# Batch 0 of a linear-attention kernel: q transposed on TensorE as loaded, kv sums on array quarters

## The chip, the cores and the metric

The kernel runs on one core of a Trainium2 chip. The time is the device time of one execution in microseconds (us); the median of several executions stands for a kernel. The engines are TensorE (PE; its weight loads are shown apart as PEld), VectorE (DVE), ScalarE (ACT), GpSimd (POOL) and SyncE (SP), which issues nearly all transfers between device memory and the on-chip memory. TensorE writes its results into PSUM, from which DVE and ACT read.

## The reference

Attention with cosine weights, followed by a feed-forward network (FFN):

```python
r = np.maximum(x, 0.0)                                   # phi, for q and for k
phi(x) = np.concatenate([r * cos_w, r * sin_w], axis=-1) # angle = pi/2 * position / S
kv  = einsum('bhsf,bhsd->bhfd', phi(k), v)
num = einsum('bhsf,bhfd->bhsd', phi(q), kv)
den = einsum('bhsf,bhf->bhs', phi(q), sum_s phi(k))[..., None] + 1e-06
x   = (num / den), heads side by side: 4608 x 512
h   = x @ w_in                                           # 512 x 2048
out = np.maximum(0.01 * h, h) @ w_out                    # 2048 x 512
```

q, k and v are float32 of 8 batches x 8 heads x 576 positions x 64. Each batch's first 512 positions are one group for the FFN (groups 0 to 7); the last 64 positions of all batches make group 8.

## The kernel before, in words

The work is a long list of named steps. A string, `ORDER`, names them in the order in which they are issued; a letter behind a colon chooses the engine of a step (D, A or P), a number behind an @ the buffer or PSUM place. Each engine, and SP with its transfers, takes its own instructions strictly in that order, so a step that waits holds everything behind it on the same engine. Several transfers can be in flight at once, but a transfer whose target buffer is still being read holds back all later ones on SP.

The steps that matter for batch 0, by their names:

- `Lq0`, `Lk0`, `Lv0`, `Lq1`, `Lk1`, `Lv1` load q, k and v of batches 0 and 1; `lq2`, `lk2`, `lv2` and so on those of later batches; `Lw1.i` and `Lw2.i` load the FFN weights in parts. Loads land in float32 staging buffers, which several of them share by turns.
- `q0.j.hg.f` (`q_prep`, lines 376 and 382): relu and one angle, cos or sin, for position slot j and four heads, from float32 to float16. `qt0.j` (`q_transpose`, line 506) turns eight heads on TensorE against a float16 identity, and `qo0.j` copies the result from PSUM to `qpT`.
- `kp0` and `kc0` do the same for k (lines 420, 376 and 382), `v0.c` casts v (line 390 or 388), all into float16. k and v are laid out so that the two heads of a pair lie on the two halves of the 128 partitions.
- `kv0.hg` (`kv_sum`, line 440): for two pairs of heads, nine matmuls for each head add up k'v in PSUM. Each takes a 64 x 128 weight (64 positions, cos and sin features side by side) on one half of the array's rows. Two extra columns of ones give the sum of k'. `ko0.hg` (`kv_out`) copies the result.
- `n0.jp.hg` (`num_half`, line 558), `N0` (`divide`, lines 534 to 539), `xt0` (line 578) and `xo0` give the numerators, the division and the transposed FFN input for two position slots and four heads.
- `f0.m` (`ffn1`, line 603) and `e0` make the first product and its activation; `F0` (`ffn2`, line 626) the second. The first two groups are computed with plain products. Groups 1 to 8 use a seven-product scheme for the second product and groups 2 to 8 also for the first (lines 740 and 823); its weight sums `T1` and `T2` are two float16 tiles that are written only after batch 1.
- `i.n` are dummy matmuls on a blank tile (line 307), 15 ahead of the first real one and nine between the first steps.

Batch 1's transposes, sums and numerators (`qt1`, `kv1`, `n1`, `xt1`) are made on TensorE between the steps `F0`; batches from 2 on have q and x transposed by DMA.

Of the kernel before, what the change touches and what calls it, by code (L numbers as in the profile page):

```python
# [13 lines left out]
P = 128  # L14
# [17 lines left out]
Lq0.0@0 q0.0.0.1:A q0.1.0.1:A Lq0.1 q0.3.0.0:P q0.2.0.1:P q0.0.0.0:A q0.1.1.0:A q0.1.1.1:A  # L32
q0.3.1.1:A q0.1.0.0:A i.0@1 Lk0.0@1 Lk0.3 Lk0.2 Lk0.1 qt0.1@0 kp0.0.1 q0.3.1.0:D q0.3.0.1:P
kc0.6:P Lv0.0@2 Lv0.2 kc0.4:D Lv0.1 kc0.1:P kp0.1.0 kp0.2.1 kp0.1.1 q0.0.1.0:A kp0.0.0 v0.0:D
kc0.8:D kc0.3:P i.2@0 qo0.1:A i.3@1 q0.2.0.0:A Lw1.0@3 v0.2:P q0.0.1.1:A qt0.0@1 i.1@0 Lv0.3
kp0.3.1 v0.3:P kc0.2:P Lw1.3 q0.2.1.0:A kc0.5:A q0.2.1.1:A qt0.2 Lw1.7 qt0.3@0 i.7@1 i.4@0
c1.0:P i.8@1 c1.3:P i.6@0 qo0.0:A Lw1.1 Lw1.2 c1.2:P Lw1.4 kc0.7:A i.9@1 i.5@0 v0.1:A kv0.0@1
qo0.3:A ko0.0:A n0.0.0@0 N0.0.0 qo0.2:A n0.1.0 N0.1.0 kc0.0:A kv0.1@1 ko0.1:A xt0.0.0@1 n0.0.1@0
N0.0.1 c1.4:P xo0.0.0:A c1.1:A Lw1.5 Lw1.6 n0.1.1 N0.1.1 Lw1.8 xt0.1.0@0 xo0.1.0:D c1.8:D c1.5:D
f0.0.a@1 f0.2.a@0 Lw2.0@0 Lq1@2 q1.0.1:D q1.3.1:D q1.3.0:D q1.2.1:D Lk1.0 kp1.0.1 Lk1.1 c1.6:P  # L40
Lw2.1@1 f0.3.a kp1.1.1 Lw2.2@3 xt0.1.1@1 f0.1.a q1.0.0:D c1.7:P f0.4.a f0.5.a Lv1.0 xt0.0.1@0
w0.0:P w1.0:P xo0.0.1:A f0.0.b f0.2.c f0.1.b xo0.1.1:A f0.0.c q1.2.0:D f0.3.c Lw2.3.0 Lw2.3.2
f0.2.d f0.3.d f0.2.e f0.3.e f0.4.d f0.5.d f0.1.c f0.0.d f0.1.d f0.0.e e0.1 kp1.0.0 q1.1.0:D
W0.1:D f0.1.e e0.0 f0.6.a@0 f0.7.a f0.6.d f0.7.d e0.3 w0.2:A f0.14@1 f0.15 e0.7 f0.8@0 lq2@0
Lv1.1 f0.9 e0.2 e0.4 f0.10@1 f0.11 e0.5 qt1.3@0 qo1.3:A kc1.2:D F0.2.0 F0.2.2 q1.1.1:A F0.0.0@0
kc1.1:A F0.1.0@1 w1.2:D qt1.0@1 qo1.0:A f0.12@0 kp1.3.1 f0.13 qt1.2@1 qo1.2:A e0.6 kp1.1.0
F0.1.2 F0.0.2 kc1.6:A kc1.5:D v1.0:D F0.1.4 w2.0:A qt1.1@1 qo1.1:A F0.0.4 kc1.8:A w2.2:P v1.2:A
v1.3:A rq2 q2.2.0:P v1.1:D q2.0.0:P q2.3.1:A F0.0.6 kp1.2.1 F0.2.4 q2.3.0:A F0.2.6 kc1.4:D
F0.1.6 kc1.0:D w3.0:D kv1.0@0 ko1.0:D w3.2:D F0.0.8 F0.2.8 F0.0.10 kc1.3:D n1.1.0@1 F0.2.10
F0.2.12 F0.2.14 F0.3.0 n1.0.0@0 F0.0.12 F0.3.2 F0.3.4 W0.2:D T1 F0.3.6 F0.3.8 F0.3.10 F0.3.12  # L50
F0.3.14 O0.3:A@1 N1.1.0 kc1.7:D kv1.1@1 O0.2:D@2 q2.2.1:P F0.1.8 N1.0.0 ko1.1:D n1.0.1@0 N1.0.1
F0.0.14 q2.1.0:A O0.0:A@3 q2.0.1:A lk2@2 rk2 ks2.0:P lv2.0@1 lv2.1 xt1.0.0@1 xo1.0.0:A n1.1.1
q2.1.1:A kc2.0:A kc2.3:A F0.1.10 lq3@3 lk3@0 F0.1.12 qT2.0 xt1.0.1@0 N1.1.1 xo1.0.1:D kc2.6:A
xt1.1.0@0 xo1.1.0:D F0.1.14 ks2.3:A xt1.1.1@0 xo1.1.1:D f1.2.0@1 f1.0.0@0 f1.0.2 f1.1.0 kc2.5:A
f1.1.2 e1.0 v2.0:A v2.1:D ks2.2:D f1.4.0 f1.4.2 f1.2.2 f1.5.0 f1.5.2 e1.2 kc2.7:A ks2.8:A f1.3.0
ks2.5:P ks2.4:P f1.10@0 f1.11 e1.5 kc2.1:D ks2.7:P ks2.6:D kc2.8:D T3 ks2.1:D kc2.4:D kc2.2:P
kv2 T2 T4 f1.6@0 ko2:A n2.0 N2.0 f1.3.2 e1.1 rk3 kc3.2:D kc3.3:A f1.7 e1.3 ks3.7:A n2.1 ks3.1:A
f1.12@1 f1.13 qT2.1 N2.1 D0.3 S1.1a n2.2 rq3 q3.2.1:A e1.6 N2.2 q3.2.0:P S1.2a f1.8@0 f1.9 n2.3
N2.3 q3.1.0:A f1.14@1 O0.1:A@0 ks3.8:P q3.1.1:D f1.15 kc3.7:P F1.2.0.0@0 W0.4:D e1.4 S1.1b
F1.1.0.0@1 lq4@1 kc3.0:A e1.7 W1.1:D S1.3b S1.1c W1.3:D S1.2c F1.1.0.1 q3.0.0:P S1.3c F1.1.1.0  # L60
q3.0.1:A S1.2b lv3.0@2 lv3.1 F1.1.1.1 F1.2.0.1 F1.2.1.0 q3.3.0:A W0.3:D M1.1:A q3.3.1:A F1.2.1.1
O1.2@1 ks3.4:D kc3.6:A F1.6.0.0@1 F1.6.0.1 F1.6.1.0 F1.6.1.1 M1.6 xT2 ks3.2:D F1.5.0.0@0
F1.5.0.1 X2.1:D f2.0.1 ks3.5:A f2.1.1 kc3.5:A kc3.4:A v3.1:A v3.0:A qT3.0 f2.0.5 S1.3a F1.7.0.0
lk4@3 W1.2:D X2.2:D ks3.3:A S1.4b X2.3:D X2.4:D W1.4:P kc3.8:A b2.0:A rq4 F1.7.0.1 F1.7.1.0
f2.0.2 ks3.6:A F1.7.1.1 rk4 s2.0:A qT3.1 f2.0.3 q4.3.0:P kc3.1:A f2.0.6 ks3.0:A kv3 kc4.4:P
u2.0:D z2.0 a2.0 f2.0.7 D0.2 ko3:A e2.0 b2.1:A q4.2.1:P f2.1.5 n3.0 S1.4a q4.0.0:P kc4.6:P
F1.5.1.0 F1.5.1.1 f2.1.6 y2.0 s2.1:A f2.1.3 N3.0 f2.0.4 ks4.7:P kc4.2:P u2.1:A M1.7 z2.1 c2.0
lv4.0@2 n3.1 F1.4.0.0 N3.1 f2.1.2 lq5@0 d2.0 f2.2.1 f2.1.7 n3.2 e2.1 O1.5@2 a2.1 b2.2:A f2.2.5
y2.1 kc4.3:A D1.5 ks4.3:A s2.2:A N3.2 f2.2.2 f2.2.6 a2.2 f2.1.4 n3.3 F1.3.0.0 N3.3 u2.2:A f2.2.3
D0.1 z2.2 v4.0:P d2.1 c2.1 S2.1a ks4.8:A e2.2 f2.3.5 ks4.5:D f2.3.1 q4.0.1:P b2.3:A F1.3.0.1  # L70
F1.3.1.0 F1.3.1.1 O1.3@2 q4.3.1:P ks4.4:D kc4.1:P f2.2.7 f2.3.6 f2.3.2 y2.2 kc4.0:A s2.3:D
F1.4.0.1 u2.3:A f2.3.7 c2.2 F2.1.0.0@0 q4.1.1:A f2.2.4 d2.2 y2.3 f2.3.3 z2.3 a2.3 F1.4.1.0 xT3
X3.1:D X3.2:D f2.3.4 d2.3 F1.4.1.1 f3.0.1 f3.1.1 O1.4@0 q4.2.0:P f3.0.5 ks4.2:A X3.3:D X3.4:D
# [75 lines left out]
def kernel(  # L149
# [751 lines left out]
    def step(name, f, *args):  # L901
        steps[name] = f, args
# [192 lines left out]
```

## Time and profile before

| | |
|---|---|
| runs | 280.63, 280.81, 281.11 us; median 280.81 |
| the profiled execution | 281.11 us, span 279.2 us |
| busy, share of the span | PE 94%, DVE 78%, ACT 65%, POOL 41% |
| granted TensorE clock | 0.999 |
| transfers | 57.59 MB, 206 GB/s over the span |

A busy row counts the time in which an engine has an instruction at work. Matmuls overlap, so the pitch of a row of matmuls (its time without the last one's duration, divided by their number less one) is what one of them costs, not its mean duration. The idle time of an engine is shown with the event that ended it. A load is read by what was waiting for it.

### The profile page before, as it was taken

The page shows a single profiled execution, that of the slowest core. Times are in us where ns is not written, and L with a number is a line of the kernel's source. Part 1 is how long each engine was busy: PE and PEld are TensorE (multiplying, and loading weights), DVE is VectorE, ACT ScalarE, POOL GpSimd, SP SyncE. Part 2 cuts the span into 40 slices and gives each one's busy share as a digit, 9 for nine tenths or more (in the row PEclk, how much of TensorE's full clock was granted, in tenths as well). Part 3 has the DMA queues.
Part 4 walks back from the last instruction along what each step waited for, and adds up shares of the span by engine and source line. Part 5 has one row for each costly group of instructions (what it writes and reads, how often), then busy time and mean ns, then how long its engine had stood idle before and what let it go on. Part 6 is the DMA issues. An engine that isn't in the chain of part 4 may idle for free.

```text
span 279.2 us, 7172 instructions
## 1 busy us (share of the span) xinstructions
PE 263.1 (94%) x2904; PEld 221.3 (79%) x2904; DVE 216.6 (78%) x430; ACT 180.6 (65%) x320; POOL 114.7 (41%) x135
## 2 busy tenths in 40 slices
PE   7669989799998999999999999999999999999993
PEld 2457445456798889998999999999999989999982
DVE  1862589594989798978988989889897888677862
ACT  7945971597996869668868557663557645666300
POOL 5854153809039930495397250970623003100000
PEclk9999999999999999999999999999999999999999
DMA  7999999779999999999795998459548214220144
GB/s 238 350 393 388 409 390 380 277 196 231 287 231 228 267 216 174 312 245 284 112 301 133 252 215 288 80 113 216 128 77 179 86 35 119 75 77 0 40 123 102
DMA packets 77263, 57.59 MB, mean 206 GB/s; under 512 B 49456, under 2 KB 65840, under 8 KB 76848
## 3 DMA queue, kind: packets, MB, share of 16 engines
q1 hardware_dynamic: 76624, 56.63, 75.5%
q10 hardware_dynamic: 608, 0.52, 0.6%
q8 instruction: 22, 0.36, 0.5%
q14 instruction: 9, 0.07, 0.1%
HBM read 36.70 MB, written 9.44 MB: 165 GB/s over the span
## 4 chain that ended last, share of the span: by engine, by line
PE 76%; DMA 12%; DVE 4%; SPq 2%; POOL 1%; issue 1%; ACT 1%
PE ps L823 32%; PE ps_f L740 27%; PE ps_h L603 5%; DMA w2st<-in_moe_w_out_dram 4%; PE ps_o L626 4%; DMA wext<-in_moe_w_in_dram 4%; PE ps_kv L440 3%; PE ps_num L523 3%; DMA out_dram<-osb 2%; DMA vst<-in_v_dram 2%; SPq L256 2%; POOL w L390 1%; PE ps_f L823 1%; DVE y L656 1%; DVE osb L656 1%
## 5 line engine op out<-in xcount | busy, mean ns | idle before, releaser
L823 PEld LDWEIGHTS <-g 128*128 128x128 f16 x640 | 61.9, 98 | 7.3 <-ACT g L612 0.2
L764 ACT ACTIVATE g<-ps_f 128x512 f16<-128x512 f32 x84 | 48.5, 596 | 26.5 <-DVE ps_f L656 14.7
L823 PE MATMUL ps<-w,g 128*128 128x256 f16 x496 | 64.4, 273 | 0.0
L740 PEld LDWEIGHTS <-w 128*128 128x128 f16 x448 | 48.4, 114 | 2.0 <-issue 1.1
L740 PE MATMUL ps_f<-xT,w 128*128 128x256 f16 x336 | 48.2, 273 | 0.0
L740 PEld LDWEIGHTS <-wext 128*128 128x128 f16 x336 | 36.4, 114 | 2.2 <-issue 1.6
L823 PE MATMUL ps<-T,ext 128*128 128x256 f16 x240 | 32.6, 272 | 0.0
L603 PE MATMUL ps_h<-xT,w 128*128 128x512 f16 (+1 forms) x144 | 29.6, 356 | 0.6 <-DVE xs L539 0.6
L823 PEld LDWEIGHTS <-ext 128*128 128x128 f16 x256 | 24.7, 98 | 2.5
L740 PE MATMUL ps_f<-X,wext 128*128 128x256 f16 x176 | 26.0, 273 | 0.2 <-ACT ps_f L388 0.2
L603 PEld LDWEIGHTS <-w 128*128 128x128 f16 x144 | 15.6, 114 | 10.6 <-DVE xs L539 0.8
L656 DVE TENSOR_TENSOR ps_f<-ps_f,u 128x512 f32<-128x512 f32 x28 | 19.5, 695 | 5.3 <-PE ps_f L740 3.2
L370 POOL TENSOR_SCALAR kst<-kst 128x2304 f32<-128x2304 f32 x6 | 13.3, 2221 | 23.5 <-DMA kst<-in_k_dram 19.3
L764 ACT ACTIVATE g<-y 128x512 f16<-128x512 f32 x28 | 17.7, 634 | 7.7 <-DVE y L656 7.7
L656 DVE TENSOR_TENSOR y<-ps_f,s 128x512 f32<-128x512 f32 x28 | 19.1, 683 | 4.1 <-PE ps_f L740 2.6
L539 DVE TENSOR_TENSOR xs<-ps_num,rden 128x512 f16<-128x512 f32 x28 | 19.4, 691 | 1.0
L612 ACT ACTIVATE g<-ps_h 128x1024 f16<-128x1024 f32 x16 | 16.2, 1024 | 4.5 <-PE ps_h L603 4.3
L823 PE MATMUL ps<-ext,g 128*128 128x256 f16 x128 | 17.9, 273 | 0.0
L656 DVE TENSOR_TENSOR osb<-ps,ext 128x512 f32<-128x512 f32 x23 | 15.6, 685 | 2.7 <-PE ps L823 1.7
L740 PE MATMUL ps_f<-xT,wext 128*128 128x256 f16 x112 | 16.8, 273 | 0.9 <-ACT s L388 0.8
L740 PE MATMUL ps_f<-X,w 128*128 128x256 f16 x112 | 16.8, 273 | 0.7 <-DVE y L656 0.6
L388 ACT COPY s<-ps_f 128x512 f32<-128x512 f32 x19 | 11.2, 587 | 9.4 <-PE ps_f L740 3.6
(121 smaller groups left out, 476.4 us busy)
## 6 DMA issues: line engine op xcount, KB each, us to landing
out_dram<-osb SPq DMA_DIRECT2D x32, 256.0 KB, 3.7
qst<-in_q_dram SPq DMA_DIRECT2D x7, 1024.0 KB, 10.6
kst<-in_k_dram SPq DMA_DIRECT2D x6, 1152.0 KB, 7.2
vst<-in_v_dram SPq DMA_DIRECT2D x12, 576.0 KB, 6.8
w2st<-in_moe_w_out_dram SPq DMA_DIRECT2D x3, 1024.0 KB, 12.9
ext<-in_moe_w_in_dram SPq DMA_DIRECT2D x4, 512.0 KB, 11.2
kst<-in_k_dram SPq DMA_DIRECT2D x4, 288.0 KB, 5.7
vst<-in_v_dram SPq DMA_DIRECT2D x4, 288.0 KB, 6.6
```

The lines of the kernel that those rows point to most:

```text
L370: POOL.tensor_scalar(out=t, in0=t, scalar1=FMAX, scalar2=0.0, op0=ALU.min, op1=ALU.max)
L388: nc.scalar.copy(o, i)
L440: nc.tensor.matmul(ps[:, o, (c - lo) * NE : (c - lo + 1) * NE], lhsT=st["kp", b][sl, c, j, :], rhs=vm[sl, c, j, :], start=(j == 0), stop=( ...
L523: nc.tensor.matmul(ps[lo:hi, h // 4, (h % 4) * NE : (h % 4 + 1) * NE], lhsT=qpT[:, h, lo:hi], rhs=kv[b][:, h, :],)
L539: nc.vector.tensor_tensor(out=xs, in0=ps[:, :, 0 : 4 * NE].rearrange("p a (b e) -> p a b e", e=NE)[:, :, :, 0:D], in1=rden.rearrange("p (a ...
L603: nc.tensor.matmul(ps[:, m % 2, lo:hi], lhsT=w1[m // 4, c][0][:, w1[m // 4, c][1], m % 4 : 512 : 4], rhs=xT[:, lo // P : hi // P, c, :], s ...
L612: nc.scalar.activation(g_tile(g)[:, 2 * i : 2 * i + 2, :], st["h", g, i], AF.Lrelu)
L626: nc.tensor.matmul(st["ps_o", g, tt], lhsT=st["g", g][:, m, tt * P : (tt + 1) * P], rhs=w2[:, m, :], start=(m == 0), stop=(m == NFT - 1),)
L656: eng.tensor_tensor(out=o, in0=a, in1=b, op=op)
L740: nc.tensor.matmul(ps[:, mi * HT : (mi + 1) * HT], lhsT=a[:, c, 2 * r0 + mi : 512 : 4], rhs=b[:, c], start=(n in (1, 5) and mi == 0 and c ...
L764: nc.scalar.activation(g_tile(g)[:, m : m + 2, r * HT : (r + 1) * HT], {"a": A, "c": y22, "e": E, "d": B_}[e].rearrange("p (m t) -> p m t" ...
L823: nc.tensor.matmul(ps[:, tt], lhsT=a[:, i, tt * P : (tt + 1) * P], rhs=b[:, i], start=(first and i == 0), stop=(i == NPR - 1 and (apart or ...
```

## The change

Only batch 0's attention is computed in another way; the whole `ORDER` string is also another one, for all groups.

- q of batch 0 is no longer prepared first. `qt0.jp.hg` (`q0_transpose`) turns float32 q as loaded, for four heads and two position slots at a time: 16 transposes of 128 x 128 into PSUM, of which a column is a position and a partition is a slot of the pair and a feature. `qo0.jp.hg.f` (`q0_out`) then does relu, angle and cast in one DVE operation out of PSUM, with a table `angles` of the cos and sin of every position; eight such operations.
- The table is made ahead by two iotas on GpSimd and two Sine operations on ACT, and lies in the space of `T1`. The float32 identity and `kvd`, a copy of kv, lie in the space of `T2`.
- Since a transposed tile now holds two position slots on the two halves of the partitions, kv is wanted on both halves. `kv0.c` (`kv0_sum`) makes it so, with four matmuls of a 64 x 64 weight where there was one of 64 x 128: two sets of features by two output halves, each on a quarter of the array, 288 in place of 72. `n0` (`num0`) adds cos and sin in two matmuls on half the rows, 64 in place of 32. `kj0` (`kv0_join`, on GpSimd) puts kv of batch 0 together for group 8.
- In the new order the four transposes `xt0` of the FFN input all stand ahead of the first `f0`; the first part of the second weights is loaded ahead of most of the first weights, into the buffer of v0; q2 is loaded ahead of the second half of k1; and 14 + 10 dummy matmuls stand in the head.

```diff
+    T1, T2 = (const.tile([P, NFT // 2, DM // 2], dt.float16, name=f"T{i}") for i in (1, 2))
+    ident32 = T2f[:, 0 : 2 * P].bitcast(dt.float32)
+    kvd = T2f[:, 2 * P : 2 * P + 2 * H * NE].rearrange("p (h s e) -> p h s e", h=H, s=2)
+    angles = T1f[:, 0 : 2 * MAIN].bitcast(dt.float32)
...
+    for s, b in enumerate((half_pi, zero)):
+        nc.scalar.activation(angles[:, s], tpos, AF.Sin, bias=b, scale=w_ang)
...
+    def q0_transpose(jp, hg):
+        ps = psum("n" if jp else "h", [P, 4, P], dt.float32, "ps_q0")
+        for hh in range(4):
+            pair = st["q", 0][:, 4 * hg + hh, 2 * jp : 2 * jp + 2, :]
+            nc.tensor.transpose(ps[:, hh, :], pair.rearrange("p j d -> p (j d)"), ident32)
+
+    def q0_out(jp, hg, f):
+        out = qpT_pair(0, jp)[:, f, 4 * hg : 4 * hg + 4]
+        nc.vector.scalar_tensor_tensor(
+            out=out, in0=st["ps_q0", jp, hg], scalar=0.0,
+            in1=angles[:, f, jp][:, None, :].broadcast_to([P, 4, P]),
+            op0=ALU.max, op1=ALU.mult)
+
+    def kv0_sum(c):
+        for f in range(2):
+            for j in range(T):
+                for o in range(2):
+                    for to in range(2):
+                        nc.tensor.matmul(
+                            ps[to * HP : (to + 1) * HP, o, lo : lo + NE],
+                            lhsT=st["kp", 0][sl, c, j, f * D : (f + 1) * D],
+                            rhs=vm[sl, c, j, :], start=(j == 0), stop=(j == T - 1))
...
+    def num0(jp, hg):
+        for hh in range(4):
+            for f in range(2):
+                for o in range(2):
+                    nc.tensor.matmul(
+                        ps[:, o, hh * NE : (hh + 1) * NE],
+                        lhsT=st["qpT2", 0, jp][sl, f, h, :],
+                        rhs=kvd[sl, h, f, :], start=(f == 0), stop=(f == 1))
```

More of the change, by code (lines that the diff above doesn't have):

```diff
@@ L38 @@
[L38 to L49, printed above, removed]
@@ new lines, in kv0_sum @@
+    def kv0_sum(c):
+        hg, cc = divmod(c, 2)
+        if cc == 0:
+            st["ps_kv0", hg] = psum("h", [P, 2, 512], dt.float32, "ps_kv")
+        ps = st["ps_kv0", hg]
+        for f in range(2):
+            lo = (2 * cc + f) * NE
+            for j in range(T):
+                for o in range(2):
+                    sl = slice(o * HP, (o + 1) * HP)
+                    for to in range(2):
+                        nc.tensor.matmul(
+                            ps[to * HP : (to + 1) * HP, o, lo : lo + NE],
+                            lhsT=st["kp", 0][sl, c, j, f * D : (f + 1) * D],
+                            rhs=vm[sl, c, j, :],
+                            start=(j == 0),
+                            stop=(j == T - 1),
+                        )
@@ new lines, in kv0_out, with kv0_join @@
+    def kv0_out(hg, eng):
+        copy(
+            eng,
+            kvd.rearrange("p (c o) s e -> p o c (s e)", o=2)[:, :, 2 * hg : 2 * hg + 2, :],
+            st["ps_kv0", hg][:, :, 0 : 4 * NE].rearrange("p o (c x) -> p o c x", c=2),
+        )
+    def kv0_join(f, eng):
+        sl = slice(f * HP, (f + 1) * HP)
+        copy(eng, kv[0][sl], kvd[sl, :, f, :])
+    def num0(jp, hg):
+        ps = psum("n" if jp else "h", [P, 2, 512], dt.float32, "ps_numh")
+        st["ps_numh", 0, jp, hg] = ps
+        for hh in range(4):
+            h = 4 * hg + hh
+            for f in range(2):
+                for o in range(2):
+                    sl = slice(o * HP, (o + 1) * HP)
+                    nc.tensor.matmul(
+                        ps[:, o, hh * NE : (hh + 1) * NE],
+                        lhsT=st["qpT2", 0, jp][sl, f, h, :],
+                        rhs=kvd[sl, h, f, :],
+                        start=(f == 0),
+                        stop=(f == 1),
+                    )
@@ L917 @@
         step(f"Lw1.{i}", load_w1, *part)
-        step(f"c1.{i}", cast_w1, *part)
+        step(f"cw.{i}", cast_w1, *part)
     for i in range(NIDLE):
@@ L931 @@
             step(f"xo0.{jp}.{hg}", x_transpose_half_out, 0, jp, hg)
-    for j in range(J):
-        step(f"qt0.{j}", q_transpose, 0, j, "n" if j == 2 else "h")
-        step(f"qo0.{j}", q_transpose_out, 0, j)
     for c in range(4):
+        step(f"kv0.{c}", kv0_sum, c)
         step(f"v0.{c}", v_pairs, 0, c, c + 1)
```

245 lines of the change are left out of this document (137 added, 108 removed).

## The prediction

> **What bounds the kernel now.** I read the page first: its totals and its 40 slices.
>
> ```profile
> span 279.2 us, 7172 instructions
> PE 263.1 (94%) x2904; PEld 221.3 (79%) x2904; DVE 216.6 (78%) x430; ACT 180.6 (65%) x320; POOL 114.7 (41%) x135
> ...
> PE   7669989799998999999999999999999999999993
> ...
> DMA  7999999779999999999795998459548214220144
> ```
>
> The profiled execution took 281.11 us for a span of 279.2, so 1.9 lie outside; the median of the runs, 280.81, is 0.3 below it. TensorE is busy almost everywhere behind slice 8; the holes are in the first 56 us, and there the DMA row is full. The view by stages (span, then busy us of PE, PEld, DVE, ACT, POOL, clock, DMA share, GB/s) says how much is left in each:
>
> ```profile
> 84.00:100.00 16.00, 14.54 (x213) 13.51 (x212) 14.07 (x25) 11.52 (x23) 16.00 (x18) 1.00 1.07 240
> 100.00:140.00 40.00, 39.43 (x505) 36.50 (x503) 35.41 (x69) 31.26 (x60) 17.02 (x21) 1.00 1.03 226
> ...
> 180.00:220.00 40.00, 39.85 (x459) 37.16 (x458) 34.48 (x71) 22.50 (x43) 15.44 (x21) 1.00 0.66 140
> ```
>
> From 84 to 220 us TensorE idles 1.46 + 0.57 + 0.15 = 2.2 us in all, so whatever the change does must be done to the head. The chain of waits there (start, us, what) runs through loads, of v, of the first and of the second weights:
>
> ```profile
> 4.31 6.57 DMA vst<-in_v_dram
> 10.90 10.55 DMA wext<-in_moe_w_in_dram
> ...
> 25.41 11.14 DMA w2st<-in_moe_w_out_dram
> ```
>
> TensorE's own timeline (start, us, what; in brackets the idle time ahead and its releaser) shows batch 0's chain and the three later holes:
>
> ```profile
> 1.17 5.55 PE L307 MATMUL ps_idle<-blank 128*128 128x512 f16 x15 [1.17 <-DVE blank L302]
> 7.81 0.62 PE L506 MATMUL ps_qt<-ident,qp 128*128 128x128 f16 x8 [1.10 <-ACT qp L376]
> ...
> 17.21 0.67 PE L558 MATMUL ps_numh<-kv,qpT 128*128 128x66 f16 x16
> ...
> 17.94 0.27 PE L603 MATMUL ps_h<-xT,w 128*128 128x256 f16 x1
> 18.85 0.63 PE L603 MATMUL ps_h<-xT,w 128*128 128x256 f16 x4 [0.64 <-DVE xs L539]
> ...
> 20.12 1.14 PE L603 MATMUL ps_h<-xT,w 128*128 128x256 f16 x5
> 21.09 0.39 PE L578 MATMUL ps_xth<-ident,xs 128*128 128x128 f16 x4
> 21.32 10.79 PE L603 MATMUL ps_h<-xT,w 128*128 128x256 f16 x62
> 32.54 0.62 PE L506 MATMUL ps_qt<-ident,qp 128*128 128x128 f16 x8 [0.43 <-DVE qp L382]
> ...
> 39.77 0.59 PE L626 MATMUL ps_o<-w,g 128*128 128x512 f16 x2 [1.39 <-POOL w L390]
> ...
> 47.11 3.61 PE L626 MATMUL ps_o<-w,g 128*128 128x512 f16 x16
> ...
> 53.50 0.42 PE L558 MATMUL ps_numh<-kv,qpT 128*128 128x66 f16 x8 [1.56 <-DVE kv L390]
> ...
> 56.83 3.43 PE L603 MATMUL ps_h<-xT,w 128*128 128x512 f16 x15
> ```
>
> The first FFN of batch 0 starts at 17.94; when the last transpose of its input is issued at 21.09, ten of its 256-wide matmuls (1.1 us) are done. From then to 56.83, where batch 1's FFN starts, TensorE loses 0.43 + 1.39 + 1.56 = 3.4 us. So its work between is 56.83 - 21.32 + 1.1 - 3.4 = 33.2 us, and the change leaves it: the same 64 + 64 wide matmuls, batch 1's transposes and sums. From 56.83 on the work is also the same. **The quantity to predict is thus when batch 1's FFN starts.** It is the later of two things: S + 33.2, with S the time at which batch 0's FFN can run in one piece, and what the loads allow.
>
> **The change, part by part.** Rows of the other engines:
>
> ```profile
> 10.08 1.51 DVE L420 SCALAR_TENSOR_TENSOR kp<-kst,sin_t 128x576 f16<-128x576 f32 x2
> 11.51 0.74 DVE L420 SCALAR_TENSOR_TENSOR kp<-kst,cos_t 128x576 f16<-128x576 f32 x1
> ...
> 13.37 0.75 DVE L420 SCALAR_TENSOR_TENSOR kp<-kst,sin_t 128x576 f16<-128x576 f32 x1
> 15.17 0.17 DVE L534 TENSOR_SCALAR den<-ps_numh 128x8 f32<-128x8 f32 x1 [1.05 <-PE ps_numh L558]
> ...
> 15.61 0.69 DVE L539 TENSOR_TENSOR xs<-ps_numh,rden 128x512 f16<-128x512 f32 x1
> 16.22 0.15 DVE L534 TENSOR_SCALAR den<-ps_numh 128x8 f32<-128x8 f32 x1
> ```
>
> ```profile
> 5.67 0.89 ACT L376 ACTIVATE qp<-qst,cos_t 128x256 f16<-128x256 f32 x2
> ...
> 12.17 0.40 ACT L376 ACTIVATE kp<-kst,cos_t 128x128 f16<-128x128 f32 x1
> 12.48 0.66 ACT L388 CAST vm<-vst 128x576 f16<-128x576 f32 x1
> 13.04 1.01 ACT L388 COPY qpT<-ps_qt 128x1024 f16<-128x1024 f16 x1
> 14.29 0.38 ACT L388 CAST kv<-ps_kv 128x264 f16<-128x264 f32 x1 [0.24 <-PE ps_kv L440]
> ...
> 17.11 0.59 ACT L388 COPY xT<-ps_xth 128x512 f16<-128x512 f16 x1
> ...
> 47.84 1.25 ACT L388 CAST vm<-ext 128x576 f16<-128x576 f32 x2 [5.69 <-DMA ext<-in_v_dram]
> ```
>
> ```profile
> 4.65 1.15 POOL L382 TENSOR_SCALAR qp<-qst,cos_t 128x256 f16<-128x256 f32 x1 [2.80 <-DMA qst<-in_q_dram]
> ...
> 8.78 3.98 POOL L382 TENSOR_SCALAR kp<-kst,cos_t 128x128 f16<-128x128 f32 x3 [0.73 <-DMA kst<-in_k_dram]
> ...
> 13.87 0.78 POOL L390 CAST vm<-vst 128x576 f16<-128x576 f32 x1 [0.50 <-DMA vst<-in_v_dram]
> ```
>
> *Removed:* 16 q preparations (12 on ACT at 0.45, 3 on POOL, 1 on DVE) and four qpT copies at 1.01: 12 x 0.45 + 4.0 = 9.4 us of ACT. That ACT is what batch 0 waits for today (the 1.10 ahead of ps_qt).
>
> *Added on DVE:* eight 128x512 operations out of PSUM. The nearest row is xs, 0.69 long, the next starting 0.61 behind: 8 x 0.61 = 4.9 us. Six kp follow one another at (11.51 - 10.08)/2 = 0.71: 4.3. In the changed order they are one queue. It starts when the first four transposes are done. Four 128x128 in float32 lie between the f16 ones' pitch (0.62 - 0.22 over 7 = 0.057 each) and that of a 512-wide matmul (3.61 - 0.38 over 15 = 0.215); I take 0.215, as the data are wider. The dummies end at about 6.4, so DVE starts at 7.5 and its last kp ends at 7.5 + 9.2 = 16.7, against 13.37 + 0.75 = 14.1 before.
>
> *Added on TensorE:* kv's 72 matmuls become 288, numh's 32 become 64. The pitch now, on array halves, is
>
> ```profile
> 63.50 1.25 PE ps_kv L440 x72
> ```
>
> 17.4 ns, against (0.67 - 0.19)/15 = 32 ns of the full-height ps_numh. On quarters it lies between 8.7 (four at once) and 32 (no overlap). I take 17.4, the nearest row: each still brings its own weight load. Here the Trainium skill pulls both ways. "TensorEngine Tiling (Array Packing)", section Key Properties, has tiles load and multiply in parallel, which would be the 8.7 end; its section Restrictions says that column tiling disables the fast weight load, which speaks for the slow end. "TensorE: Matmul & The Clock Gate", section "Wait — 56ns, not 53.3ns?", has no start-to-start below about 25 ns; the 17.4 of this trace is already under that, and by 25 the sum would be 288 x 7.6 ns = 2.2 us worse than mine, 283.9.
>
> *S, step by step.* kv's first half needs four qo and four kp (7.5 + 2.4 + 2.8 = 12.7) and v: start 13.0, 144 x 17.4 ns and 0.2 to drain, 15.7. Copy on ACT, 264 to 528 columns, 0.24 + 0.59: 16.5. Behind it ACT makes four kc at 12.48 - 12.17 = 0.31: 17.8, which the second half waits for (DVE's 16.7 is earlier). Second half 20.5; copy 21.3; numh 32 on halves, the first 16 by 21.8; two normalisations, 0.2 + 1.13 and 1.05: 24.2; two groups of input transposes, now all ahead of the FFN: **S = 24.5**. So FFN of batch 1: 24.5 + 33.2 = 57.7, **+0.9 us** on 56.83, if the 3.4 us of holes all close.
>
> *Loads.* The bytes from v0's landing (13.87) to v1's second half (47.84) are w1 3.93, w2 4.19, q1 1.05, k1 1.18, q2 1.05, v1 1.18 = 12.6 MB in 34.0 us: 370 GB/s. The changed order has the same bytes ahead of v1, so v1 cannot come sooner; w2's last half comes 11.4 MB behind 13.87, at 44.7, cast 45.5. Behind that TensorE still has 32 wide matmuls (6.9), batch 1's sums (1.4), numerators (1.0) and transposes (0.9): 55.7. One thing adds to it: w2's first load now takes v0's buffer, so on SP it waits for POOL's last v cast, at 13.2 + 0.6 + 0.7 to 1.3 (kp, alone or as in the 3.98 row) + 0.7 = 15.2 to 15.9, and all later weights queue behind. The loads ahead run dry at 13.87 + 1.05/0.37 = 16.7. The first half of q, issued at about 0.7, landed at 4.65, of which 0.52/0.37 = 1.4 is streaming: up to 2.5 us before data flow. So the hole is 0 to 1.7; I take 0.9: 56.6, still under 57.7.
>
> *Costed at nothing:* the angle table (two Sine operations of 128x256, 0.45 each by the ACT row) runs before ACT has work; without that cover, 0.9. POOL's two iotas fit before 4.65. Batch 0's two kv joins on POOL, at most 0.8 each, are wanted only by the last group and by a weight sum. The rest of the order is a new plan too: later TensorE stalls can fall by at most 2.2; I take no change.
>
> Sum against the profiled execution: 281.11 + 0.9 = 282.0; against the median **281.7**.
>
> **Rivals.**
> - *Faster: quarters overlap, and the hole in the loads is nil.* S falls by 288 x 8.7 ns = 2.5 to 22.0, 55.2; loads bind at 55.7: -1.1, 279.7; fewer stalls behind, as low as 279. For it: 9.4 us of ACT freed. Against: loads full already.
> - *It does not matter: quarters overlap, but the loads bind with their hole.* 56.6 against 56.83: 280.6.
> - *Slower: quarters don't overlap.* It decides once the pitch passes 17.4: at 32 ns, S is 288 x 14.4 = 4.1 later, 285.8. For it: 64-column weight loads, which no row shows; against, the halves overlap.
> - *A new wait in the later plan*, of the size of the 1.39 above: 283.1. DVE at 14.07 of 16 from 84 to 100 leaves room for one.
>
> **How the numbers follow.** Forecast 0.38 (of this 0.10 within 0.2%, about the 0.56 us that a measurement here can tell); faster rival 0.26; "does not matter" 0.12 (0.08 within, 0.04 faster); no overlap 0.14; later wait 0.10. Faster 0.30, same 0.18, slower 0.52. The range, 279.0 to 285.0, runs from the faster rival to short of the 32 ns end; the forecast's own is 280.9 to 282.6.
>
> **What would show it.** In the changed profile: kv's rows, 288, at a pitch of 17 ns; DVE's eight operations of about 0.69, last kp near 16.7; batch 0's FFN in one piece from about 24.5; no wait for a w2 cast above 1 us; batch 1's FFN at about 57.7. Wrong would be S before 23 or after 26, a DMA share well under 1 near 16 us for over 2 us, or a TensorE idle behind 57 us that differs from 2.2 by over 1.

## The result: 9.4 us slower, and the profile after

The changed kernel takes 290.12 us (289.45 to 290.46), the kernel before on the same chip 280.72 (280.36 to 281.11): a ratio of 1.031, interval 1.027 to 1.035. The forecast was 281.7 with a range to 285.0: the direction was right, the size was far off, and the time lies outside the range. The profiled execution took 289.98 us with a span of 288.1, 8.9 over the span before.

The page of the changed kernel (totals, the slices of TensorE, its clock and the transfers, and the queue that carries instructions):

```profile
span 288.1 us, 7645 instructions
PE 267.7 (93%) x3136; PEld 225.8 (78%) x3136; DVE 223.6 (78%) x430; ACT 174.6 (61%) x307; POOL 118.0 (41%) x142
...
PE   8644999999998999999999899999999999999992
...
PEclk9955799999999999999999999999999999999997
...
q8 instruction: 24, 0.39, 0.6%
```

A slice is 7.2 us. In slices 2 to 4 TensorE is busy 6, 4 and 4 tenths, and in slices 3 and 4 its clock is at 5 tenths; before, the clock was full throughout. TensorE's timeline names the idle time (the DVE rows below it are from DVE's own timeline):

```profile
11.44 0.78 PE L554 MATMUL ps_kv<-vm,kp 64*64 64x66 f16 x72
...
14.29 0.70 PE L582 MATMUL ps_numh<-T,qpT 64*128 64x66 f16 x32 [0.88 <-ACT T L403]
15.86 0.32 PE L554 MATMUL ps_kv<-vm,kp 64*64 64x66 f16 x6 [0.86 <-DVE qpT L533]
17.35 1.98 PE L554 MATMUL ps_kv<-vm,kp 64*64 64x66 f16 x128 [1.17 <-issue]
24.10 0.37 PE L554 MATMUL ps_kv<-vm,kp 64*64 64x66 f16 x10 [4.77 <-issue]
...
28.87 7.98 PE L685 MATMUL ps_h<-xT,w 128*128 128x256 f16 x44
...
63.54 0.81 PE L685 MATMUL ps_h<-xT,w 128*128 128x512 f16 x3
```

```profile
6.85 2.48 DVE L533 SCALAR_TENSOR_TENSOR qpT<-ps_q,T 128x512 f16<-128x512 f32 x4 [4.95 <-PE ps_q L529]
...
15.63 0.74 DVE L435 SCALAR_TENSOR_TENSOR kp<-kst,sin_t 128x576 f16<-128x576 f32 x1
```

In the middle of kv's second half TensorE stops twice, for 1.17 and 4.77 us. Nothing in the profile releases it ("issue"): no semaphore, no data. Between the two stops lie 128 matmuls, which with their 128 weight loads are 256 instructions. The stages of two microseconds (PE, PEld, DVE, ACT, POOL, clock, DMA share, GB/s) show what runs beside it:

```profile
14.00:16.00 2.00, 0.85 (x38) 0.75 (x37) 2.00 (x4) 1.42 (x5) 1.70 (x3) 0.84 0.66 246
16.00:18.00 2.00, 0.83 (x54) 0.69 (x54) 1.86 (x7) 0.00 (x0) 0.00 (x0) 0.50 0.55 148
...
20.00:22.00 2.00, 0.00 (x0) 0.00 (x0) 0.00 (x0) 0.00 (x0) 1.22 (x2) 0.50 0.93 295
22.00:24.00 2.00, 0.00 (x0) 0.00 (x0) 0.00 (x0) 0.00 (x0) 0.43 (x1) 0.50 0.98 310
```

From 20 to 24 us TensorE does nothing while the DMA engines are nearly full (shares 0.93 and 0.98). The clock falls ahead of both stops: taken in steps of 0.1 us it is at 0.50 from 15.35 to 32.4 us, and in the 3.35 us ahead of its fall TensorE was busy for 1.70, with no hole longer than 0.88.

The budget: batch 1's FFN starts at 63.54 in place of 56.83, **+6.7**, and what lies behind it lasts 288.1 - 63.54 = 224.6 in place of 222.4, **+2.2**; together the 8.9.

**Theory** (in the expectations below the instruction or supply theory). TensorE's instructions come to it in blocks of 256 over the same DMA engines as the data. It uses up a block of quarter matmuls in 2 us (the row of 128, at half clock) and then waits for the next at the border of the two blocks. The count of packets on the instruction queue fits: 2 x 3136 TensorE instructions / 256 = 24.5, and the queue carried 24; the kernel before has 2 x 2904 / 256 = 22.7 and carried 22:

```profile
q8 instruction: 22, 0.36, 0.5%
```

In the changed kernel two of these packets lie in the stretches 14.75 to 15.0 and 21.75 to 22.0 us, and none between; TensorE goes on 2.1 to 2.6 us behind each. For these two stretches (data queue and instruction queue: packets, MB, share of the DMA engines):

```profile
q1 hardware_dynamic: 40, 0.07, 77.5%
q8 instruction: 1, 0.02, 26.1%
```

```profile
q1 hardware_dynamic: 38, 0.08, 113.3%
q8 instruction: 1, 0.02, 23.5%
```

That this queue is TensorE's alone is inferred from the counts. The Trainium skill, "Runtime: NRT & Kernel Launch", section "Instruction fetch mechanics", also has blocks of 256 instructions, fetched while the one before is executed; it calls the cost of a border mostly hidden. Here it was not: the two stops are 5.9 us.

**Rivals:** quarters or 64-column weights are slow in themselves; the loss comes from late loads; or from the new order, which fits badly.

### The profile page after: what moved, and what is told of

The parts are those of the page before. It is cut to its first block, busy times and chain, and to the rows that moved or that the text cites. A ratio compares the mean times of both kernels' runs of the same rounds, so it can differ in the third digit from the quotient of the medians.

```text
span 288.1 us, 7645 instructions
## 1 busy us (share of the span) xinstructions
PE 267.7 (93%) x3136; PEld 225.8 (78%) x3136; DVE 223.6 (78%) x430; ACT 174.6 (61%) x307; POOL 118.0 (41%) x142
## 5 line engine op out<-in xcount | busy, mean ns | idle before, releaser
L906 PE MATMUL ps<-w,g 128*128 128x256 f16 x496 | 65.1, 273 | 0.9 <-DVE ext L737 0.9
L823 PEld LDWEIGHTS <-w 128*128 128x128 f16 x448 | 48.4, 114 | 1.8 <-DVE u L405 0.5
L823 PE MATMUL ps_f<-xT,w 128*128 128x256 f16 x336 | 48.9, 273 | 0.3 <-DVE u L405 0.3
L906 PE MATMUL ps<-T,ext 128*128 128x256 f16 x240 | 31.9, 273 | 0.7 <-ACT osb L403 0.7
L685 PE MATMUL ps_h<-xT,w 128*128 128x512 f16 (+1 forms) x144 | 30.9, 373 | 0.0
L685 PEld LDWEIGHTS <-w 128*128 128x128 f16 x144 | 16.5, 119 | 11.1
L385 POOL TENSOR_SCALAR kst<-kst 128x2304 f32<-128x2304 f32 x6 | 12.8, 2136 | 18.3 <-DMA kst<-in_k_dram 17.8
L393 POOL TENSOR_SCALAR kp<-kst,sin_t 128x256 f16<-128x256 f32 x29 | 17.0, 594 | 6.9 <-DVE osb L405 6.6
L385 POOL TENSOR_SCALAR qst<-qst 128x2048 f32<-128x2048 f32 x6 | 11.8, 1963 | 15.1 <-DMA qst<-in_q_dram 15.1
L906 PE MATMUL ps<-ext,g 128*128 128x256 f16 x128 | 17.4, 272 | 0.0
```

Source lines behind the costliest of these rows:

```text
L385: POOL.tensor_scalar(out=t, in0=t, scalar1=FMAX, scalar2=0.0, op0=ALU.min, op1=ALU.max)
L393: eng.tensor_scalar(out=o, in0=i, scalar1=col, scalar2=1.0, op0=ALU.mult, op1=ALU.mult)
L685: nc.tensor.matmul(ps[:, m % 2, lo:hi], lhsT=w1[m // 4, c][0][:, w1[m // 4, c][1], m % 4 : 512 : 4], rhs=xT[:, lo // P : hi // P, c, :], s ...
L823: nc.tensor.matmul(ps[:, mi * HT : (mi + 1) * HT], lhsT=a[:, c, 2 * r0 + mi : 512 : 4], rhs=b[:, c], start=(n in (1, 5) and mi == 0 and c ...
L906: nc.tensor.matmul(ps[:, tt], lhsT=a[:, i, tt * P : (tt + 1) * P], rhs=b[:, i], start=(first and i == 0), stop=(i == NPR - 1 and (apart or ...
```

## The experiments

**1. Halves in place of quarters, in the changed kernel.**

```diff
-  four 64x64 matmuls a position slot (kv0_sum), one copy
+  ps[:, o, lo:lo+NE] <- lhsT=kp[sl, c, j, :], 64x128, as before
+  four ACT copies of 64x264 into kvd
```

> The changed kernel with kv of batch 0 summed as before (72 matmuls of 64x128 on array halves) and its copy out of PSUM made four times, twice across the partition halves, so that all else of the change stays. Instruction theory (TensorE's instructions arrive in blocks of 256, and in the head a block takes 5 to 7 us, so a stretch that uses a block up faster stands still): no idle time ended by issue above 0.5 us ahead of kv's matmuls, granted clock 1.00 from 14 to 35 us, batch 1's FFN at 57 +- 1 instead of 63.5, time 282 to 284. Order theory (the new order of loads and steps costs the time): 288 or more, batch 1's FFN still behind 62.

284.93 us, ratio 1.010 (1.001 to 1.019). No wait by issue is left, so the supply theory holds that far, but the time missed its 282 to 284, batch 1's FFN starts at 60.82 and not at 57, and the clock fell all the same. TensorE's rows, and a row of SP's waits (who waited for what: us in total, times, longest):

```profile
17.12 1.17 PE L552 MATMUL ps_kv<-vm,kp 64*128 64x66 f16 x36 [0.25 <-ACT kp L391]
...
23.57 8.98 PE L689 MATMUL ps_h<-xT,w 128*128 128x256 f16 x44
...
52.26 0.74 PE L455 MATMUL ps_kv<-vm,kp 64*128 64x66 f16 x36 [1.52 <-POOL vm L405]
...
60.82 5.34 PE L689 MATMUL ps_h<-xT,w 128*128 128x512 f16 x24
```

```profile
SPq L245 <- DMA w2st<-in_moe_w_out_dram: 8.8, 1, 8.8
```

Batch 1's sums wait for v1, whose load stood on SP behind q2's, which waited 8.8 us for w2's second part to leave its buffer. The clock was at 0.50 from 15.25 to 28.9 us; it fell inside an idle stretch of 2.1 us. A second limit lies right under the first.

**2. The kernel before with its kv summed four times** (the first three sums are overwritten), so 288 matmuls on halves.

```diff
+            for _ in range(4 if b == 0 else 1):
                 for j in range(T):
```

> The kernel before with batch 0's kv summed four times over (288 matmuls of 64x128 on array halves, the first three rounds overwritten); nothing on quarters. Instruction theory: TensorE stands still with issue as the reason inside ps_numh's first 16 (after some 8) and in the second kv half after about 119 matmuls, together 4 to 8 us; the clock falls under 0.8 between 14 and 28 us; time 286 to 291. Quarter theory (the standstill belongs to 64x64 tiles): no such idle time, only the 216 more matmuls at 17 ns, 3.8 us in the chain, of which the later holes of 3.4 take a part: 281 to 285.

293.17 us in a single run, above its 286 to 291.

```profile
19.90 3.55 PE L441 MATMUL ps_kv<-vm,kp 64*128 64x66 f16 x128 [1.90 <-issue]
26.37 0.36 PE L441 MATMUL ps_kv<-vm,kp 64*128 64x66 f16 x9 [2.92 <-issue]
```

The same stops, again 128 matmuls apart, without a quarter in the kernel: it is the number of instructions, not the geometry. The first stop came 15 matmuls later than expected, and 4.1 of the 12.1 us that the span gained lie behind batch 1's FFN (64.83), 3.84 of them in one wait on DVE at 97.87.

**3. Seven dummies fewer ahead of kv, in the changed kernel.**

```diff
- i.6@0 i.7@1 i.8@0 i.4@1 i.1@0 i.9@1 i.5@0 kv0.0@0
+ kv0.0@0
```

> The changed kernel without the seven dummy matmuls just ahead of kv (14 instructions fewer). Instruction theory: the two idle times move by seven matmuls within the second kv half, from behind its 6th and 134th to behind its 13th and 141st, and the time stays within 1.5 us of 290. Quarter theory and any theory of data: they stay behind the 6th and the 134th.

```profile
16.31 0.29 PE L553 MATMUL ps_kv<-vm,kp 64*64 64x66 f16 x13 [0.86 <-DVE qpT L532]
17.67 1.98 PE L553 MATMUL ps_kv<-vm,kp 64*64 64x66 f16 x128 [1.07 <-issue]
24.68 0.27 PE L553 MATMUL ps_kv<-vm,kp 64*64 64x66 f16 x3 [5.04 <-issue]
```

The first stop comes behind 13 matmuls in place of 6, the second leaves 3 in place of 10: both moved by exactly the seven taken away. A place in the instruction stream sets the stops, no event of another engine. The time, 289.18 in a single run, hardly moved.

**4. All weight loads from w2's first part on held till kv is done.**

```diff
- Lw1.4 Lw2.0@2 w0.0:P Lw1.1 Lw1.2 cw.1:P cw.2:P
- n0.0.0@0 Lw1.5 Lw1.6
+ n0.0.0@0
+ ko0.1:A hold Lw2.0@2 w0.0:P Lw1.1 Lw1.2 cw.1:P cw.2:P Lw1.5 Lw1.6
+    def hold():  # a small copy on SP that waits for batch 0's kv copy
+        nc.sync.dma_start(held, kvd[:, H - 1, 0, 0:64])
```

> The changed kernel with the weight loads from w2's first part on held on SP until batch 0's kv is copied out (a small transfer that reads kv stands ahead of them), so that TensorE's instruction blocks meet no data from about 16.5 us on. If the block's wait is that for a place among data packets: the second idle time in kv falls from 4.8 to under 2.5 us, and kv ends before 21.5 instead of 24.5. If a block takes its time whatever else is in flight: it stays above 4 us. Time 289 to 293 either way, since weights come later.

```profile
17.55 1.98 PE L443 MATMUL ps_kv<-vm,kp 64*64 64x66 f16 x128 [0.55 <-issue]
21.28 0.37 PE L443 MATMUL ps_kv<-vm,kp 64*64 64x66 f16 x10 [1.75 <-issue]
```

```profile
18.00:20.00 2.00, 1.52 (x112) 1.39 (x102) 1.21 (x4) 0.00 (x0) 0.00 (x0) 0.50 0.04 8
```

With the DMA engines nearly idle (share 0.04) the stops shrink to 0.55 and 1.75 us. So most of the 4.77 is waiting behind data, and some of it is there without data: the packets of the instruction queue move at 15.0, 18.6 and 22.9 us, 3.6 and 4.3 apart, where the two of the changed kernel are 6.9 apart, and TensorE still goes on 2.4 to 2.7 us behind the first two. The kernel as a whole is no faster (292.74 in a single run): TensorE waits 4.50 us for a w1 cast ahead of batch 0's FFN, as the weights come late.

**5. Batch 0's kv on quarters in the kernel before**, 144 matmuls in place of 72, nothing else.

```diff
+ for f in range(2 if b == 0 else 1):
+     fs = slice(f * HP, (f + 1) * HP) if b == 0 else slice(0, P)
-     ps[:, o, ...] <- lhsT=st["kp", b][sl, c, j, :]
+     ps[fs, o, ...] <- lhsT=st["kp", b][sl, c, j, fs]
```

> The kernel before, with batch 0's kv sums alone on array quarters: each 64x128 weight becomes two of 64x64, so 144 matmuls in place of 72; nothing else changes, the result is the same. It tells the price of a quarter from the price of the number of instructions. Supply theory: the work ahead of the first 144 fits the blocks already there; the next border lies some 14 matmuls behind the end of kv's second half (counted from the fourfold run's borders), so kv itself has no wait with releaser issue, its half of 72 lasts about 72 x 8 to 17 ns = 0.6 to 1.3 us, and a wait of 0.5 to 3 us with releaser issue stands behind it, in numh or the first input transposes; time 281 to 285. Geometry theory (64-column weights are slow, or quarters wait for each other): kv's rows themselves are at over 17 ns, no wait by issue; time by what kv loses. No theory: under 280.

284.04 us in a single run, beside 281.81 (279.53 to 284.15) for the kernel before; the time alone shows no difference.

```profile
13.50 0.78 PE L442 MATMUL ps_kv<-vm,kp 64*64 64x66 f16 x72
...
17.32 0.26 PE L560 MATMUL ps_numh<-kv,qpT 128*128 128x66 f16 x3 [0.17 <-ACT kv L388]
19.91 0.59 PE L560 MATMUL ps_numh<-kv,qpT 128*128 128x66 f16 x13 [2.33 <-issue]
```

A quarter matmul costs (0.78 - 0.19)/71 = 8.3 ns, half of the 17.4 on halves: quarters do overlap four ways. Yet 72 more of them bring a stop of 2.33 us in numh, seven matmuls behind the end of kv, where the count of instructions had put it at some 14.

**6. Run 1 with 17 more dummies in its idle stretches.**

```diff
+ I.0 (9 dummies) behind kv0.1, I.1 (4) behind kv0.3, I.2 (4) ahead of the last xt0
```

> The changed kernel with batch 0's kv summed once on array halves and copied to both partition halves (as in the run on halves), and 17 dummy matmuls more on TensorE: nine behind the first two pairs' kv, four behind the last two pairs', four ahead of the last group of input transposes, where that run had it idle 2.10, 0.84 and 0.85 us. Clock theory: the half clock of 16 to 28 us in the run on halves came from those holes; with them filled the clock stays at 0.9 to 1.0, batch 0's FFN of 44 wide-256 matmuls takes 6 to 7 us in place of 8.98, and TensorE reaches the first F0 (32.4 there) 2 to 4 us sooner. Whether the time follows: if the work bounds, 281 to 283; loads theory: v of batch 1, whose load stands behind q2's wait on SP for the cast of w2's second part, still comes at about 50 us, batch 1's FFN stays at 60 to 61, and the time at 284 to 285.

286.15 us, ratio 1.017 (1.012 to 1.022), no better than run 1 and a little above the 284 to 285 of the loads theory.

```profile
52.42 0.75 PE L455 MATMUL ps_kv<-vm,kp 64*128 64x66 f16 x36 [2.08 <-POOL vm L405]
...
60.99 5.34 PE L689 MATMUL ps_h<-xT,w 128*128 128x512 f16 x24
```

The clock stayed at 1.00 through the head, and batch 1's FFN starts where it did. Batch 0's FFN starts at 22.30 here, and 33.2 us of work and 4.95 us of waits for casts of w1, w2 and v1 (0.91, 1.01, 0.67, 0.28, 2.08) lead to 60.45: in the new order the loads and their casts alone put it at 61.

**7. Run 6 with the load of w2's first part behind all of w1's.**

```diff
- Lw1.4 Lw2.0@2 w0.0:P Lw1.1
+ Lw1.4 Lw1.1
- Lw1.8 xo0.0.0:A
+ Lw1.8 Lw2.0@2 xo0.0.0:A
- cw.7:P xo0.0.1:A
+ cw.7:P w0.0:P xo0.0.1:A
```

> The filled run on halves, with the load of w2's first part (and its cast) moved behind all of w1's, so that SP no longer waits at 8 to 15.7 us for v0's buffer with w1 queued behind. Loads theory (v1's landing sets batch 1's FFN, at 61.0 in the filled run, and the hole at 14 to 18 us is part of why v1 lands at 50): DMA share from 14 to 18 near 1.0 (0.77 and 0.59 there), v1's first cast at 47.5 to 48.8 in place of 50.1, batch 1's FFN 1.3 to 2.5 sooner, 58.5 to 59.7; time 1 to 2.5 us under the filled run's. If the loads do not bind: FFN at 61 as there, and only the weight waits of 0.91 and 1.01 ahead of batch 0's FFN change.

287.63 us, ratio 1.025 (1.021 to 1.030). The hole in the loads is gone (DMA share 1.05 from 14 to 20 us) and v1's first cast moves from 50.1 to 47.45, as expected, but batch 1's FFN starts at 62.07 and not at 58.5 to 59.7, as a new wait eats the gain:

```profile
28.83 6.56 PE L689 MATMUL ps_h<-xT,w 128*128 128x256 f16 x32 [5.41 <-ACT xT L403]
```

ACT's cast of that part, which waits 5.44 us for the load, stands ahead of the copies of batch 0's FFN input; the later load now holds them.

**8. Run 6 with q2 loaded behind v1.**

```diff
- w0.2:A lq2@0 cw.7:P
+ w0.2:A cw.7:P
- Lv1.0 kp1.1.1 rq2 v1.0:P
+ Lv1.0 kp1.1.1 v1.0:P
- Lv1.1 f0.3.a
+ Lv1.1 lq2@0 rq2 f0.3.a
```

> As the filled run on halves, and q2 of batch 2 loaded behind v1 in place of ahead of k1's second half (with its relu). In the run on halves q2's load waited 8.8 us on SP for w2's second part, with k1, w2's last part and v1 behind it. Loads theory: v1 now lands some 3 to 8 us sooner, the waits ahead of batch 1's sums go, and batch 1's FFN starts at 57 to 58.5; time 280 to 282. Work theory (the loads did not bind): the same as the filled run within 0.5 us. A later wait of batch 2 for its q would show as a TensorE wait on q's transpose at 75 to 90 us; I expect none.

291.28 us, ratio 1.031 (1.024 to 1.037), far from the 280 to 282. I had overlooked one step: q2's relu still stood on POOL ahead of two casts of v1, which so waited for q2, and TensorE lost 4.76 us on v1.

**9. Both moves together,** the relu now behind v1's casts.

```diff
+ the moves of run 7, and lq2@0 behind Lv1.1 as in run 8
+ v1.3:P rq2 (relu of q2 behind the last cast of v1 on POOL)
+ v1.1:A behind qo1.0:A; q2.0.1:A q2.0.0:A q2.1.1:A behind qo1.1:A
```

> As the run before it, and q2 loaded behind v1, now with its relu on POOL behind v1's last cast and with ACT's part of v1's casts and of q2's preparation in that order too (in the first trial the relu stood ahead of two v1 casts, which waited for it till 53.7). Loads theory: no wait of 6 to 9 us on SP for w2's second part, v1's first cast at 45 to 46.5, and batch 1's FFN at 56.8 to 58.5, now set by TensorE's own work; time 279.5 to 282. A wait of batch 2 for its q would show ahead of its numerators at 80 to 90 us.

288.45 us, ratio 1.029 (1.025 to 1.033). v1's first cast is at 43.0, sooner than expected, but the wait of run 7 is still there, 6.19 us, and the time missed its 279.5 to 282.

**10. Both moves in the changed kernel, with its quarters.**

```diff
  the changed kernel, and the moves of run 9
```

> The changed kernel with the same two moves of loads and nothing else: its kv on quarters, 288 matmuls, stays. Supply theory (in the changed kernel TensorE's missing instructions and the half clock behind them bind, and the loads, though late, are no more than the second limit, about 2.5 us below): the waits with releaser issue of 1 to 1.5 and 4 to 6 us stay, the clock is 0.50 from about 17 to 30, batch 1's FFN stays at 62.5 to 64, time 288 to 291. Loads theory of the whole loss: FFN at 57 to 60, time 283 to 286.

289.71 us in a single run. The stops stay (2.08 and 4.22 us) at a DMA share of 1.05, and batch 1's FFN starts at 65.0 although three of v1's four casts are done by 46, so late loads do not make the loss. Run 9's wait for w2 is not in it: ACT's cast of that part starts at 29.50 without one, as the stops have taken the time. Run 9, with this wait, can't serve to price the quarters.

**11. Run 9 with ACT's and POOL's casts of w2's first part behind the last copies of the FFN input.**

```diff
- w0.2:A cw.7:P w0.0:P xo0.0.1:A
+ cw.7:P xo0.0.1:A
- cw.5:A cw.6:P
+ cw.5:A w0.2:A cw.6:P w0.0:P
```

> The run with both loads moved, with ACT's and POOL's casts of w2's first part put behind the last copies of batch 0's FFN input and behind the last casts of w1; before, ACT held those copies for 6.19 us till that part had landed. With the loads full from 10 us on, no wait by issue and TensorE busy, this says what the way on halves is worth when nothing else is in its way. If the chain to batch 0's FFN and TensorE's own work bind: no wait of over 1 us ahead of batch 0's FFN, its 44 matmuls within 7 us, batch 1's FFN at 56 to 58, time 279 to 281.5, at the kernel before within 0.5%. If the late part of w2 or a load still binds, a wait of 1 to 4 us on w2st stands in the first F0 or on ext ahead of batch 1's sums, and the time is 282 to 285.

285.68 us, ratio 1.017 (1.012 to 1.021). The time is above the 279 to 281.5 expected. Batch 0's FFN starts at 22.00 and no longer stops behind its first part, but the cast holds the first activations, and with them PSUM: TensorE waits 3.65 us in the FFN, and its clock falls again.

**12. Run 11 with this cast behind two activations.**

```diff
- cw.5:A w0.2:A cw.6:P
+ cw.5:A cw.6:P
- e0.0 F0.1.0@0
+ e0.0 w0.2:A F0.1.0@0
```

> The run before it with one step moved: ACT's cast of the second half of w2's first part stands behind the first two activations of batch 0's FFN in place of ahead of them. In that run ACT waited 3.49 us for this part, the activations behind it held two PSUM places, TensorE lost 3.65 us and its clock fell to half from 28 to 35 us. Theory: batch 0's FFN now runs in one piece from 22.0 at clock 1.00, no TensorE wait above 1.5 us ahead of batch 1's FFN, which starts at 22.0 + 33.2 = 55.2 to 56.5; time 278.5 to 280.5, the first version of this way that is not slower than the kernel before. Rival: another wait takes its place (F0 for w2's first part, or batch 1's sums for v1), batch 1's FFN at 57 to 60, time 281 to 284.

284.97 us, ratio 1.016 (1.011 to 1.021), which is the rival's case. The FFN runs in one piece, 44 matmuls in 6.25 us from 22.43, and the next wait shows:

```profile
51.79 1.04 PE L644 MATMUL ps_numh<-kv,qpT 128*128 128x66 f16 x16 [2.93 <-ACT kv L403]
```

ACT's preparation of q2, which comes late since its load stands behind v1, waits 3.82 us for POOL's relu and holds batch 1's kv copy. On halves, each run from 7 on moved a load or a cast and met the next instruction in line on an in-order engine.

**13 and 14. The same order, cleared of these waits, once with halves and once with quarters.**

```diff
  run 12, and:
- q2.0.1:A q2.0.0:A q2.1.1:A (ahead of kc1.7:A), q2.2.0:A
+ all four behind kc1.5:A
  run 14: the changed kernel's q, kv and numerators in this order, without the 17 dummies
```

> The run before it (halves, dummies, both loads moved, w2's casts aside) with ACT's four preparations of q2 put behind k1's last ones; there they waited 3.82 us for POOL's relu of q2 and held the copy of batch 1's kv, for which TensorE waited 2.93 us at half clock afterwards. TensorE was at batch 1's first kv at 47.15 there, and from kv to batch 1's FFN it has 8.6 us of work. If nothing else binds: batch 1's FFN at 55.2 to 56.5, time 278.5 to 280.5, at or under the kernel before: then the way with float32 transposes is worth about 1 us, and all of the loss of the changed kernel came from the quarters' instructions and the order. Rival: k1's preparations on ACT or a cast of v1 on POOL hold batch 1's second sums: FFN at 57 to 59, time 280.5 to 283.

> The changed kernel's quarters, 288 matmuls, in the order of the run beside it (without its 17 more dummies). Supply theory: waits by issue of 1 to 2.5 and 4 to 6 us in kv's second half, clock 0.50 from about 17 to 31, batch 0's FFN from 28.5 to 29.5 (22.4 with halves), batch 1's FFN 61.5 to 64 though v1 is cast by 46; time 286 to 289, 6 to 8 us over the run beside it. Order theory (the order's waits made the loss, and the quarters' stall is hidden by the loads): within 2 us of the run beside it.

Halves: **280.85 us**, ratio 1.002 (0.998 to 1.006), no difference from the kernel before. Quarters: **289.43**, ratio 1.031 (1.027 to 1.036). TensorE's rows, first with halves:

```profile
16.32 0.74 PE L552 MATMUL ps_kv<-vm,kp 64*128 64x66 f16 x36 [0.62 <-ACT kp L391]
...
21.87 6.25 PE L689 MATMUL ps_h<-xT,w 128*128 128x256 f16 x44
28.80 0.59 PE L712 MATMUL ps_o<-w,g 128*128 128x512 f16 x2 [0.68 <-POOL w L405]
...
55.86 6.21 PE L689 MATMUL ps_h<-xT,w 128*128 128x512 f16 x28
```

then with quarters:

```profile
18.19 1.97 PE L554 MATMUL ps_kv<-vm,kp 64*64 64x66 f16 x128 [1.93 <-issue]
24.39 0.37 PE L554 MATMUL ps_kv<-vm,kp 64*64 64x66 f16 x10 [4.23 <-issue]
...
29.17 8.17 PE L685 MATMUL ps_h<-xT,w 128*128 128x256 f16 x44
...
64.02 6.21 PE L685 MATMUL ps_h<-xT,w 128*128 128x512 f16 x28
```

The stages from 21 to 28 us, halves and then quarters, show clock 1.00 against 0.50 under equally full loads:

```profile
21.00:28.00 7.00, 6.94 (x54) 5.38 (x53) 1.56 (x2) 5.12 (x7) 2.32 (x3) 1.00 1.06 390
```

```profile
21.00:28.00 7.00, 2.40 (x50) 2.00 (x50) 1.74 (x6) 1.50 (x3) 2.80 (x4) 0.50 1.05 387
```

In this order the quarters (with the dummies and copies that differ) cost 289.43 - 280.85 = 8.6 us. In the spans, 287.6 - 279.0, the same 8.6: 64.02 - 55.86 = 8.2 till batch 1's FFN and 0.4 behind it. The parts of the 8.2: the stops are 1.93 + 4.23 = 6.2, and the 44 matmuls at the lower clock 8.17 - 6.25 = 1.9; the other steps ahead of the FFN take 1.1 more (29.17 - 21.87 = 7.3, less the 6.2), and 1.0 goes off again, with 0.68 for the wait that only halves have.

Two limits of this comparison. The clock in run 14 fell at 16.03 us, ahead of the first stop, and run 13 has dummies in just these holes; no run has quarters with the dummies, so how much of the lower clock belongs to the quarters is not shown. And 8.6 is the price once all else is cleared away. In the changed kernel's own order the quarters cost 290.12 - 284.93 = 5.2 us (run 1), and without them the order's late weights and v1 still cost 1.0 to 1.7% (runs 1 and 6): the two limits overlap.

## Why the prediction was wrong

The profiled execution took 289.98 us, 8.0 over the sum of 282.0. Of these, 63.54 - 57.7 = 5.8 lie ahead of batch 1's FFN and 2.2 behind its start.

- **What bounds the kernel: right.** S + 33.2 holds. In the changed kernel the FFN starts at 28.87 and loses 7.98 - 6.25 = 1.7 to the clock: 28.87 + 1.7 + 33.2 = 63.8, measured 63.54. In run 13, 21.87 + 33.2 + 0.68 of wait = 55.75, measured 55.86.
- **"S, step by step": the step that failed.** "Second half 20.5" counted data and pitch alone; the half ended at 24.10 + 0.37 = 24.5. The 1.17 + 4.77 us for instructions were in no term, no rival and no bound of the range. The sum knew that TensorE gets 216 + 32 more matmuls and as many weight loads, and asked only how long each runs, not how they reach the engine. The half clock, 0.50 from 15.35 us on, was not in it either. The rest of the chain was faster than forecast: kv's first half started at 11.44 in place of 13.0, its second at 15.86 in place of 17.8. Without the stops, S would have been about 28.87 - 5.94 = 22.9, under my 24.5. So the direction, slower, came out right by luck: the terms behind its 0.9 us were too long, and one that was not there made the loss.
- **The pitch: mis-sized in the other direction.** 17.4 ns taken, 8.3 measured at full clock, at the overlapped end. "TensorEngine Tiling (Array Packing)" of the Trainium skill, Key Properties, was right on this end, and the 25 ns of "TensorE: Matmul & The Clock Gate", section "Wait — 56ns, not 53.3ns?", as a floor from start to start does not hold for array tiles.
- **Added on DVE: right.** Eight operations at 2.48/4 = 0.62 us; the last kp ends at 15.63 + 0.74 = 16.4, 16.7 was forecast. The float32 transposes cost less than the 0.215 us taken for each: eight took 1.04 us.
- **Loads: wrong where it did not decide.** The hole was at the bad end of the 0 to 1.7 (DMA share 0.66 and 0.55 in place of 1.05 over 4 us, 1.8 us). But "loads bind at 56.6" was too early by 4.4: it put 10.2 us of TensorE work behind w2's last part, while in this order v1 comes behind that, its sums start at 52.42 (run 6), and 8.6 us of work follow to 60.99. Without the stops the time would have been near that of run 1, 285, at the end of the range, and the forecast still too low.
- **"From 56.83 on the work is also the same": wrong by 2.2 us.** The traces say where they lie. TensorE is idle for 3.0 us behind 63.54, before 2.2; new are a wait of 0.68 on ACT at 121.38 and one of 0.94 on DVE at 161.72, neither of which run 1 has in the same later order; why they come stays open. It is busy for 0.6 more. Its last matmul ends 5.5 us ahead of the end of the span, before 4.6. These 0.8 us are in runs 1, 13 and 14 too. All data are through by 286.0, but a packet of a second instruction queue, q14, still comes at 287.5 to 287.75; the kernel before has none there within its span. That the end waits for this packet is likely, but not shown.
- **The rivals.** None named the mechanism. "Faster", the way with overlapping quarters, had the pitch right, and its S of 22.0 is near run 13's 21.87, which is partly luck, as that run has halves, more dummies and another order. There the way ends level with the kernel before, not at 279.7: of the 1.0 us won at batch 1's FFN 0.8 is given back, in the longer tail. No version here beats the kernel before.

## What to carry over

Splitting matmuls into smaller tiles multiplies instructions, weight loads included, and the supply of instructions is a resource like any other: count how many lie in each few microseconds and look whether they outrun the blocks that come through a DMA system full of data. A wait "by issue" in the middle of a run of equal matmuls, with 256 instructions to the next such wait, is its mark. When a load or cast is moved on in-order engines, look at every instruction behind it: here every move on halves met a new wait until the whole line was clear.

## What the hardware showed that was not expected

- A border between blocks of 256 instructions cost TensorE 1.1 to 5.0 us in the loaded head, and still 0.55 and 1.75 us with the DMA engines nearly idle. The changed kernel's matmuls have no other wait by issue; over its whole span a block lasts 288.1 / 24.5 = 11.8 us on average.
- Four 64x64 tiles gave a pitch of 8.3 ns at full clock.
- The granted clock, once down, stayed at 0.50 for whole multiples of 3.41 us: 3.41 (runs 2, 5 and 7), 6.83 (runs 8, 9, 11 and 12), 13.65 (run 1), 17.07 (the changed kernel, runs 3, 10 and 14) and 20.48 (run 4). No long hole was needed: in the changed kernel it fell when TensorE had been busy for 1.70 of the last 3.35 us, its longest hole 0.88, and in run 14 for 1.54 of 3.35. With dummies in these holes (runs 6 and 13) it stayed at 1.00; in run 13 TensorE was busy for 2.98 us from 12.65 to 16.0. The busy share alone doesn't set it, as the kernel before kept 1.00 with 1.33 busy in the 3.4 us from 7.0. "The HAM clock gate" section of the Trainium skill's "TensorE: Matmul & The Clock Gate" has the same half clock behind an idle window of about 3.4 us. The length agrees; that the window must be idle does not, as TensorE was busy for half of it.
